# Sums of product weights from on-chip float16 parts instead of a kept float32 copy, with a new weight layout and moved steps

## Chip, cores and metric

One core of one Trainium2 chip runs the whole program. The metric is the device time of one execution in microseconds (us); before the change it is 1241.75 us, the median of three runs (1240.58 to 1242.31). The engines are TensorE (PE, with its weight loads PEld), VectorE (DVE), ScalarE (ACT), GpSimd (POOL) and SyncE (SP), which issues all DMAs here. Each engine works through its own program in order.

## The reference

Attention with a sigmoid in place of the softmax over 8 batches of 12 heads (448 positions, head size 64), whose output, as 3584 rows of 768, goes through two matrix products with an ELU between them. The two weight matrices arrive as float64.

```python
scores = scale * np.matmul(q, k.transpose(0, 1, 3, 2)) - np.log(S)
attn = 1.0 / (1.0 + np.exp(-scores))
x = np.matmul(attn, v)            # -> rows of B*S, 768 columns
h = x @ w_in                      # 768 x 2048, float64 on input
g = np.where(h > 0.0, h, np.exp(np.minimum(h, 0.0)) - 1.0)
return (g @ w_out).astype(np.float32)
```

## The kernel before

Every large product runs on float16 pairs: a value is split into a high and a low float16 part, and high x high, high x low and low x high are added up in PSUM.

**Stages in the order of time.** From 0 to about 140 us the attention of batches 0 and 1 runs while w_in arrives in eight units of 256 columns; each unit is turned from float64 words into float32 (tile `stage`) and then into float16 parts (tile `wi`). To 197 us the first layer of batch 0 runs (`ph`), to 283 us its second layer (`po`) as 96 steps X0 to X95 of three matmuls, while w_out is loaded and split (tiles `wo`, `to`, `so`). Then come the first layer of batch 1 (to about 346 us) and the attention of batch 2 (to about 442 us), with the second layer of the batch before as filling. From there on each batch 2 to 7 has a stage of blocks, in which the first layer is done by a scheme of seven products (k = 1 to 7) on half-size blocks, four times over (w = 0 to 3), 28 products n = 0 to 27 in the order of the table `USES`; then the attention of the next batch, filled with the second layer of this one. The last second layer ends the program.

**The weights of the seven products.** Three of the seven (slots 4, 5, 6 of `blend` in DRAM) are plain quarters of w_in, stored from `wi` by the step W of each unit (`store_parts`, L344, six DMAs of 96 KB). The other four are sums and differences of quarters. For them the float32 unit is stored to a DRAM tile `kept` (step t, L315, 768 KB), read back in four parts into `room` (L358, 192 KB each), added on DVE (L363), split into a high part on ACT (L369) and a low part on DVE (L372), and stored to `blend` (L379). One step K is one piece of that chain (`make_sums`); the split parts lie in a ring of three buffers, so that a fourth split waits for the store of the first.

**What sets the order.** The first stage follows a hand-written table `ORDER` of tokens: l, A to F, t are steps of a unit of w_in; S, G, V the scores, sigmoid and values of a pair of heads; X, W, K as above. `A` (L220) writes the float32 buffer of a unit, of which there are two, so A of unit u+2 waits until everything that reads unit u is done: F (L310) and the store t. The later stages follow `order`, for the first layer of batch 1, and `order_of_blocks`, which say after which product the next pair of heads is measured (`measure_next`: two reductions over the raw q, k, v on DVE and a short chain to the tile `dg`), scaled (`scale_next`: a matmul `pb` on `dg`, a short chain on DVE, then POOL) and split (`split_step`). `behind` hangs the evaluation behind each product: copies on ACT, `exps` and `rests` (the ELU), and the split of g.

Of the kernel before, what the change touches and what calls it, by code (L numbers as in the profile page):

```python
# [11 lines left out]
F32 = mybir.dt.float32  # L12
# [41 lines left out]
X79 K X80 K O4 X81 X82 K X83 K X84 X85 K X86 K X87 X88 K X89 K X90 X91 K X92 K X93 X94 K
X95 K O5
# [11 lines left out]
def attention_ffn(  # L67
# [12 lines left out]
    P = 128  # L80
# [41 lines left out]
    wi = space.rearrange("p (j c f) -> p j c f", j=2, c=NK)  # L122
    BLOCK = 2 * HK * 2 * P
    blend = dram.tile([NW, 7, P, BLOCK], F16, name="blend")
    kept = dram.tile([NF // WF, P, NK * WF * P], F32, name="kept")
# [137 lines left out]
    def load_w_in(u):  # L263

        src = w_in.rearrange("(c p) f -> p c f", p=P)
        if not stage:
            stage.append(
                sb.tile([P, WR * 2 + WT, NK, WF * P], F32, tag="wo", name="stage")
            )
        if u < NF // WF:  # L270
            st = stage[0][:, u % WR * 2 : u % WR * 2 + 2]
            st = st.rearrange("p a c x -> p (a c x)").rearrange("p (c x) -> p c x", c=NK)
            queue = nc.sync
            queue.dma_start(st.bitcast(U64), src[:, :, u * WF * P : (u + 1) * WF * P])
            w_in_words[u] = words(st)
# [3 lines left out]
    def w_in_parts(u):  # L279

        st, both = {}, w_in_both.setdefault(u // 2, {})
        d = wi[:, :, :, u * WF * P : (u + 1) * WF * P]
# [8 lines left out]
        def sums():  # L291
# [3 lines left out]
            top = st["t"].bitcast(BF16).rearrange("p a (c t) -> p a c t", t=2)[:, :, :, 1]  # L295
            for c in range(NK):
                nc.tensor.matmul(
                    to, ones_in, top[:, c], start=u % 2 == 0 and c == 0,
                    stop=c == NK - 1, skip_group_check=True,
                )  # L300
# [13 lines left out]
        def keep():  # L314
            nc.sync.dma_start(kept[u], st["t"].rearrange("p c x -> p (c x)"))  # L315

# [10 lines left out]
            "t": keep,  # L327
# [9 lines left out]
    def store_parts(u):  # L337

        w, j = divmod(u, 2)
        for slot, c, odd in ((4, 0, 0), (5, HK, 0), (6, HK, 1)):  # L340
            dst = blend[w, slot].rearrange("p (j c h x) -> p j h c x", j=2, c=HK, h=2)
            for h in range(2):
                f = (u * WF + odd) * P
                nc.sync.dma_start(dst[:, j, h], wi[:, h, c : c + HK, f : f + P])  # L344

    def sums_of_parts():

        names = "22", "21", "11", "12"
# [5 lines left out]
        def load(u, *xs):  # L354
            src = kept[u].rearrange("p (c x) -> p c x", c=NK)
            for x in xs:
                c, f = HK * (x[1] == "2"), P * (x[0] == "2")
                nc.sync.dma_start(  # L358
# [1255 lines left out]
```

## Time and profile before

| | before |
|---|---|
| median of three runs | 1241.75 us |
| the profiled execution | 1241.87 us |
| its span, first to last instruction | 1240.1 us |
| PE busy | 1130.4 us (91%) |
| DVE busy | 853.8 us (69%) |
| ACT busy | 708.6 us (57%) |
| DMA engines, mean rate | 143 GB/s |

The profiled execution takes 1.8 us more than its span, and lies 0.1 us above the median. PE has the largest share, so what counts is where PE stands idle (some 110 us) or runs below its full clock, and on what it waits there. Shares of the whole span say little: the stages have different limits.

### The profile page before, as it was taken

The numbers are of one execution on the slowest core, as the hardware profiler recorded it, in microseconds if no ns is written. First come the engines' busy times: TensorE is split into PE (matmuls) and PEld (weight loads), VectorE is DVE, ScalarE is ACT, GpSimd is POOL, SyncE is SP. The second block draws the span as 40 slices with busy tenths as digits, with TensorE's granted clock in tenths as the row PEclk, the third lists the DMA queues.
The fourth block names the chain that finished last, engine by engine and source line by source line (L and its number), as shares of the span: only waits on it lengthen the run. The fifth ranks groups of instructions, "written<-read, shape, count | busy, mean of one in ns | idle before, by whom it ended". The sixth has DMA issues, their size and how long they took to land.

```text
span 1240.1 us, 22359 instructions
## 1 busy us (share of the span) xinstructions
PE 1130.4 (91%) x8626; PEld 718.5 (58%) x8626; DVE 853.8 (69%) x1767; ACT 708.6 (57%) x983; POOL 70.0 (6%) x276
## 2 busy tenths in 40 slices
PE   6668997488998899999999998999999999999998
PEld 2223453244554479556965588557955588558965
DVE  2657787376888558787877668787877678776600
ACT  4668766153575546676566644776566545775400
POOL 0000000010000000010100000010001000010000
PEclk9889999698999999999999999999999999999999
DMA  9776647443535738443854248363844268324200
GB/s 222 195 241 203 215 130 182 127 135 115 125 102 125 215 107 251 131 99 99 255 148 104 63 141 247 105 119 121 248 129 94 57 179 259 76 62 149 89 26 26
DMA packets 258267, 177.24 MB, mean 143 GB/s; under 512 B 189552, under 2 KB 225392, under 8 KB 258160
## 3 DMA queue, kind: packets, MB, share of 16 engines
q1 hardware_dynamic: 258160, 175.82, 51.3%
q8 instruction: 67, 1.10, 0.4%
q14 instruction: 40, 0.33, 0.1%
HBM read 130.94 MB, written 28.31 MB: 128 GB/s over the span
## 4 chain that ended last, share of the span: by engine, by line
PE 59%; DVE 17%; DMA 9%; ACT 7%; SPq 4%; issue 4%; POOL 0%; DVEq 0%; ACTq 0%; POOLq 0%
PE po L1099 23%; PE psc L655 8%; PE ph L899 7%; PE pav L713 6%; PE X L998 5%; PE po_r L1099 4%; DMA qk<-nat 3%; SPq L344 2%; DVE g L1036 2%; DMA room<-kept 1%; DMA kept<-stage 1%; DMA wi<-blend 1%; PE pav L731 1%; DVE mt L211 1%; DVE wi L772 1%
## 5 line engine op out<-in xcount | busy, mean ns | idle before, releaser
L1099 PE MATMUL po<-wo,g 128*128 128x384 f16 x2304 | 392.1, 329 | 10.4 <-DVE wo L478 4.5
L1099 PEld LDWEIGHTS <-g 128*128 128x128 f16 x2688 | 258.3, 98 | 201.0 <-issue 35.8
L998 PEld LDWEIGHTS <-wi 128*128 128x128 f16 x3024 | 287.9, 98 | 28.0 <-issue 19.6
L700 DVE SCALAR_TENSOR_TENSOR at<-sg,at 128x896 f16<-128x896 f32 x126 | 132.5, 1087 | 76.9 <-ACT at L699 76.6
L998 PE MATMUL X<-wi 128*128 128x224 f16 x1296 | 133.0, 259 | 10.1 <-DVE c L1047 10.1
L679 ACT ACTIVATE sg<-psc,bias,sc 128x896 f32<-128x896 f32 x108 | 114.1, 1090 | 31.6 <-PE psc L655 31.5
L655 PE MATMUL psc<-qk 64*128 64x448 f16 (+2 forms) x960 | 110.8, 382 | 8.4 <-ACT qk L1283 3.7
L899 PE MATMUL ph<-xh,wi 128*128 128x448 f16 x576 | 114.2, 359 | 0.0
L699 ACT ACTIVATE at<-sg 128x896 f16<-128x896 f32 x126 | 113.4, 945 | 0.6
L618 ACT ACTIVATE nat<-raw,sc 128x384 f16<-128x384 f32 (+1 forms) x108 | 52.2, 535 | 79.4 <-POOL sc L589 74.5
L899 PEld LDWEIGHTS <-wi 128*128 128x128 f16 x576 | 56.7, 99 | 59.1 <-issue 8.9
L621 DVE SCALAR_TENSOR_TENSOR nat<-raw,sc,nat 128x384 f16<-128x384 f32 (+1 forms) x108 | 52.4, 526 | 28.1 <-ACT nat L618 27.4
L713 PE MATMUL pav<-at,vn 128*64 128x448 f16 x648 | 68.2, 355 | 1.1 <-DVE al L193 1.1
L1099 PE MATMUL po_r<-wo,g 128*128 128x384 f16 x384 | 64.3, 326 | 0.0
L1012 ACT ACTIVATE eb<-c,msc 128x896 f32<-128x896 f32 x24 | 25.0, 1042 | 65.4 <-DVE c L1047 65.4
L655 PEld LDWEIGHTS <-qk 64*128 64x128 f16 (+1 forms) x864 | 30.7, 98 | 53.5 <-issue 34.9
L1109 DVE TENSOR_SCALAR o<-po,osc 128x384 f32<-128x384 f32 x48 | 29.3, 611 | 41.0 <-PE po L1099 38.1
L713 PEld LDWEIGHTS <-vn 128*64 128x64 f16 x648 | 34.0, 110 | 33.3 <-issue 14.5
L998 PE MATMUL Y<-xh,wi 128*128 128x224 f16 x432 | 45.3, 259 | 2.7 <-DVE wi L772 2.7
L998 PE MATMUL X<-xh,wi 128*128 128x224 f16 x432 | 45.4, 259 | 0.8 <-DVE ea L1017 0.8
L679 ACT ACTIVATE sg<-psc,bias 128x896 f32<-128x896 f32 x42 | 41.3, 1008 | 8.3 <-PE psc L655 7.8
L998 PE MATMUL A<-xh,wi 128*128 128x224 f16 x432 | 45.3, 259 | 0.0
(162 smaller groups left out, 1396.6 us busy)
## 6 DMA issues: line engine op xcount, KB each, us to landing
wi<-blend SPq DMA_DIRECT2D x168, 384.0 KB, 4.2
stage<-in_moe_w_in_dram SPq DMA_DIRECT2D x8, 1536.0 KB, 8.7
wo<-in_moe_w_out_dram SPq DMA_DIRECT2D x13, 768.0 KB, 4.7
raw<-in_q_dram SPq DMA_DIRECT2D x96, 96.0 KB, 3.4
raw<-in_k_dram SPq DMA_DIRECT2D x96, 96.0 KB, 2.9
out_dram<-o SPq DMA_DIRECT2D x48, 192.0 KB, 1.9
rv<-in_v_dram SPq DMA_DIRECT2D x36, 192.0 KB, 2.7
kept<-stage SPq DMA_DIRECT2D x8, 768.0 KB, 5.4
```

Source lines behind the costliest of these rows:

```text
L618: nc.scalar.mul(hi, src, s)
L621: nc.vector.scalar_tensor_tensor(lo, src, s, hi, op0=ALU.mult, op1=ALU.subtract)
L655: nc.tensor.matmul(psc[:, j, :S] if g < NC else psc[rows[x], j, :S], kk[rows[j], o], qq[rows[j], :S], start=(n == 0), stop=(n == n_parts - 1),
L679: a = nc.scalar.activation(sg, psc[:, :, :S], AF.Sigmoid, bias=bias, scale=scale)
L699: nc.scalar.mul(parts[0], sg, 2.0**ATOP)
L700: nc.vector.scalar_tensor_tensor(parts[1], sg, 2.0**ATOP, parts[0], op0=ALU.mult, op1=ALU.subtract)
L713: nc.tensor.matmul(pav[rows[j], :S], vv[i][:, j * NC + g if g < NC else 2 * NC + j], sg[k][:, j], start=(g == 0 and n == 0), stop=False,)
L899: nc.tensor.matmul(ph[:, :S], wi[:, wj, c, f * P : (f + 1) * P], hidden_of(b, c)[:, xj], start=(n == 0), stop=(n == 3 * NK - 1),)
L998: nc.tensor.matmul(to[:, j * HS : (j + 1) * HS], block[:, j, c, wj], rhs(k, c, xj), start=(k in (1, 5) and j == 0 and n == 0), stop=(j == ...
L1012: a = nc.scalar.activation(e, src, AF.Exp, scale=m[:, 0, 4 * w : 4 * w + 1])
L1099: nc.tensor.matmul(po[:, :HM], lh(gj, f), wo[:, i, f, wj], start=(n == 0), stop=(n == 3 * NF - 1),)
L1109: nc.vector.tensor_scalar(o, po[:, :HM], sc, None, op0=ALU.mult)
```

## The change

- The store t and the DRAM tile `kept` are gone, and the 32 loads from it. `whole_of` adds the float16 parts of `wi` into `room` on DVE instead, 768 columns at a time, twice a unit. High and low parts are then a copy on ACT and a subtraction on DVE, without the factor. A unit has eight steps K as before; before X95 there are 29 of them instead of 31, from X14 on.
- `wi` lies by unit (last unit first), block and part. A unit of w_in comes in two DMAs (runs of 1 KB) instead of one (2 KB). W stores a unit in two DMAs with runs of 1536 bytes instead of six with 256.
- W0 to W7 stand from X62 to X91 instead of X0 to X7.
- In the stage of blocks the scaling stands after n = 5 and 17 instead of 4 and 14; the second measurement (n = 22) goes to the attention behind it, after the first pair's third sigmoid; the measurement at f = 10 in `order` goes too. The scale of the batch and the first ELU stand behind the product (1,1) instead of (2,0). The tables of Exp and Sigmoid are loaded by a one-element activation, behind (5,0) and behind the last ELU. The split of the blocked x is ordered anew (`finish_first`, `finish_second`).

```diff
-            queue.dma_start(st.bitcast(U64), src[:, :, u * WF * P : (u + 1) * WF * P])
+            for i in range(WF):
+                f = (u * WF + i) * P
+                nc.sync.dma_start(st[:, i * NK : (i + 1) * NK].bitcast(U64), src[:, :, f : f + P])
...
-        def keep():
-            nc.sync.dma_start(kept[u], st["t"].rearrange("p c x -> p (c x)"))
...
-        for slot, c, odd in ((4, 0, 0), (5, HK, 0), (6, HK, 1)):
-            dst = blend[w, slot].rearrange("p (j c h x) -> p j h c x", j=2, c=HK, h=2)
-            for h in range(2):
-                f = (u * WF + odd) * P
-                nc.sync.dma_start(dst[:, j, h], wi[:, h, c : c + HK, f : f + P])
+        for slot, n, a in ((4, 2, 0), (6, 1, 3 * HK)):
+            nc.sync.dma_start(
+                blend[w, slot : slot + n].rearrange("s p (j x) -> p s j x", j=2)[:, :, j],
+                wi[:, NU - 1 - u, a : a + n * HK].rearrange("p (s c) h x -> p s (c h x)", s=n),
+            )
...
-        def load(u, *xs):
-            src = kept[u].rearrange("p (c x) -> p c x", c=NK)
...
+        def whole_of(u, i):
+            x = room[:, 2 * i : 2 * i + 2].bitcast(F32).rearrange("p b (c x) -> p (b c) x", x=P)
+            hi, lo = (wi[:, NU - 1 - u, i * NK : (i + 1) * NK, h] for h in range(2))
+            nc.vector.tensor_tensor(x, hi, lo, op=ALU.add)
...
-            nc.scalar.mul(parts(i)[:, 0], one[x].rearrange("p (c x) -> p c x", c=HK), scale)
+            nc.scalar.copy(parts(i)[:, 0], one[x].rearrange("p (c x) -> p c x", c=HK))
...
+            elif k == 1 and w == 1:
+                first()
+                start_of_a()
             elif k == 5:
                 nc.scalar.copy(s5, bank(5, w))
+                if not w:
+                    nc.scalar.activation(warm, bias, AF.Exp)
...
             elif k == 4:
                 exps(st["e1"][:, 1], x, w)
                 rests(st["e1"][:, 1], x, w)
+                if w == NW - 1:
+                    nc.scalar.activation(warm, bias, AF.Sigmoid)
...
     order_of_blocks = {
-        4: scale_next, 7: split_step, 8: split_step, 9: split_step, 11: split_step, 12: measure_next,
-        14: scale_next, 18: split_step, 19: split_step, 20: split_step, 21: split_step, 22: measure_next,
+        5: scale_next, 7: split_step, 8: split_step, 9: split_step, 11: split_step, 12: measure_next,
+        17: scale_next, 18: split_step, 19: split_step, 20: split_step, 21: split_step,
     }
...
                 p.sigmoid(2)
+                if hp == 0:
+                    measure_next()
```

How the order of instructions moves is shown for three places. A row is the line, the operation, out<-in, the shape, and how many stand in a row.

SP, the queue that issues the DMAs, around X0 before the change (`wo` is w_out on its way in, `so` its low words):

```order
L446 DMA wo<-in_moe_w_out_dram 128x2x384 x12
L344 DMA blend<-wi 128x3x128 x48
L358 DMA room<-kept 128x3x128 x4
L446 DMA wo<-in_moe_w_out_dram 128x2x384
L1111 DMA out_dram<-o_0_0_1664 128x384
L441 DMA so_13_1708<-in_moe_w_out_dram 128x384
```

The same place in the changed kernel:

```order
L434 DMA wo<-in_moe_w_out_dram 128x2x384 x13
L1114 DMA out_dram<-o_0_0_1610 128x384
L429 DMA so_13_1652<-in_moe_w_out_dram 128x384
L1114 DMA out_dram<-o_1_0_1674 128x384
L429 DMA so_14_1681<-in_moe_w_out_dram 128x384
```

The 48 stores and four loads that stood ahead of the thirteenth load of w_out are gone from there. Further on in the same queue, from about X60, stores of sums (L373) and of the plain quarters (L338) now alternate:

```order
L373 DMA blend<-room 128x768 x2
L338 DMA blend<-wi 128x2x768
L338 DMA blend<-wi 128x768
L373 DMA blend<-room 128x768 x2
L1114 DMA out_dram<-o_0_1_1859 128x384
L338 DMA blend<-wi 128x2x768
L338 DMA blend<-wi 128x768
L338 DMA blend<-wi 128x2x768
L338 DMA blend<-wi 128x768
L373 DMA blend<-room 128x768 x2
```

So the stores of plain quarters are now queued among those of the sums on which the ring of three waits.

DVE from X62 to the scale of batch 1 (L868), before: L363 is a sum, L372 a low part, L1109 empties an output tile.

```order
L363 TENSOR_TENSOR room<-room 128x384 x2
L1109 TENSOR_SCALAR o_0_1_1914<-po_0_1_1825,osc_1399 128x384
L363 TENSOR_TENSOR room<-room 128x384 x2
L372 SCALAR_TENSOR_TENSOR room<-room,wr 128x3x128 x4
L363 TENSOR_TENSOR room<-room 128x384 x4
L372 SCALAR_TENSOR_TENSOR room<-room,wr 128x3x128 x2
L1109 TENSOR_SCALAR o_1_1_1994<-po_1_1_1908,osc_1399 128x384
L372 SCALAR_TENSOR_TENSOR room<-room,wr 128x3x128 x2
L363 TENSOR_TENSOR room<-room 128x384 x4
L372 SCALAR_TENSOR_TENSOR room<-room,wr 128x3x128 x3
L1109 TENSOR_SCALAR o_2_1_2068<-po_2_1_1987,osc_1399 128x384
L868 TENSOR_REDUCE mx_95<-xs_445 128x1
```

The same stretch after: L354 is the new `whole_of`, L357 a sum, L366 a low part, L1112 an output tile.

```order
L354 TENSOR_TENSOR room<-wi 128x768 x2
L357 TENSOR_TENSOR room<-room 128x384 x4
L366 TENSOR_TENSOR room<-room 128x3x128 x4
L354 TENSOR_TENSOR room<-wi 128x768 x2
L357 TENSOR_TENSOR room<-room 128x384 x2
L1112 TENSOR_SCALAR o_1_1_1941<-po_1_1_1851,osc_1398 128x384
L357 TENSOR_TENSOR room<-room 128x384 x2
L366 TENSOR_TENSOR room<-room 128x3x128 x4
L354 TENSOR_TENSOR room<-wi 128x768 x2
L357 TENSOR_TENSOR room<-room 128x384 x4
L366 TENSOR_TENSOR room<-room 128x3x128
L1112 TENSOR_SCALAR o_2_1_2018<-po_2_1_1935,osc_1398 128x384
```

Six instructions of 768 columns have come in, and nine low parts stand where eleven stood.

DVE in the stage of blocks of batch 4, around n = 22, before: L211 to L183 are the measurement of pair 2, L1017 and L1036 belong to the ELU and the split of g.

```order
L1017 SCALAR_TENSOR_TENSOR ea_2_7865<-X_2_7672,msc_7351,ea_2_7865 128x448
L211 TENSOR_REDUCE mx_93<-rv_97 128x1
L211 TENSOR_REDUCE mt_2_8004<-raw_2_7695 128x7
L578 TENSOR_REDUCE mx_93<-mt_2_8004 128x2
L581 TENSOR_TENSOR mx_93<-mx_93,mt_2_8004 64x1 x2
L179 STREAM_TRANSPOSE tr<-mx_93 128x32
L181 TENSOR_REDUCE trm<-tr 128x1
L183 TENSOR_SCALAR dg<-blocks,trm 128x12
L1036 SCALAR_TENSOR_TENSOR g<-eb_2_7942,msc_7351,g 128x4x224
L1016 TENSOR_SCALAR ea_3_8057<-ea_3_8057 128x448
```

After the change those rows stand behind the stage of blocks, in the attention (L688 is the second half of a sigmoid):

```order
L1031 SCALAR_TENSOR_TENSOR g<-eb_3_8049,msc_7309,g 128x4x224
L1031 SCALAR_TENSOR_TENSOR g<-ea_3_8000,msc_7309,g 128x2x224
L688 SCALAR_TENSOR_TENSOR at_0_8118<-sg_0_8091,at_0_8118 128x896
L688 SCALAR_TENSOR_TENSOR at_0_8121<-sg_0_8116,at_0_8121 128x896
L210 TENSOR_REDUCE mx_92<-rv_96 128x1
L210 TENSOR_REDUCE mt_2_8152<-raw_2_7651 128x7
L566 TENSOR_REDUCE mx_92<-mt_2_8152 128x2
L569 TENSOR_TENSOR mx_92<-mx_92,mt_2_8152 64x1 x2
L178 STREAM_TRANSPOSE tr<-mx_92 128x32
L180 TENSOR_REDUCE trm<-tr 128x1
L182 TENSOR_SCALAR dg<-blocks,trm 128x12
```

The measurement no longer splits the evaluation of the blocks; it now stands between the sigmoids of the first pair.

## Rows read from the trace of the kernel before

**Rows 1.** Windows: length, busy PE, PEld, DVE, ACT, POOL, PE clock, DMA share, GB/s

```profile
60.00:80.00 20.00, 12.15 (x54) 3.85 (x51) 9.30 (x15) 10.77 (x10) 0.00 (x0) 0.83 0.95 289
200.00:220.00 20.00, 8.97 (x51) 4.75 (x50) 10.66 (x18) 6.70 (x12) 0.00 (x0) 0.89 0.90 190
220.00:240.00 20.00, 4.50 (x17) 2.21 (x17) 5.55 (x10) 4.10 (x7) 0.00 (x0) 0.52 0.48 131
```

**Rows 2.** Timeline of ACT: start, duration, line, operation [idle before <-releaser]

```profile
51.50 1.58 ACT L220 ACTIVATE stage<-stage 128x1536 f32<-128x1536 f32 x1 [5.60 <-DMA kept<-stage]
...
64.12 1.01 ACT L679 ACTIVATE sg<-psc,bias 128x896 f32<-128x896 f32 x1 [0.21 <-PE psc L655]
...
71.85 1.58 ACT L220 ACTIVATE stage<-stage 128x1536 f32<-128x1536 f32 x1 [6.72 <-DMA kept<-stage]
```

**Rows 3.** Timeline of DVE and of PE in the same stretch

```profile
45.03 1.82 DVE L310 SCALAR_TENSOR_TENSOR wi<-stage,swi,wi 128x1536 f16<-128x1536 f32 x1 [0.62 <-ACT wi L325]
...
74.39 1.86 PE L655 MATMUL psc<-early 64*128 64x448 f32 x4 [6.82 <-ACT sg L679]
```

**Rows 4.** Timeline of SP's queue: start and duration of issuing

```profile
61.35 0.54 SPq L315 DMA_DIRECT2D kept<-stage  x1
...
195.84 27.83 SPq L344 DMA_DIRECT2D blend<-wi  x48
...
226.53 0.42 SPq L446 DMA_DIRECT2D wo<-in_moe_w_out_dram  x1
```

**Rows 5.** Timeline of DVE, PE and ACT around X0

```profile
204.38 0.96 DVE L249 SCALAR_TENSOR_TENSOR wo<-wo 128x768 uint32<-128x768 uint32 x1
...
210.25 2.48 PE L1099 MATMUL po<-wo,g 128*128 128x384 f16 x14 [1.07 <-DVE wo L478]
...
232.81 0.88 ACT L228 ACTIVATE wo<-wo 128x768 uint32<-128x768 uint16 x1 [23.67 <-DMA wo<-in_moe_w_out_dram]
...
235.50 0.80 PE L242 MATMUL so<-wo,ones 128*128 128x384 bf16 x2 [22.77 <-DVE wo L233]
236.10 4.71 PE L1099 MATMUL po<-wo,g 128*128 128x384 f16 x18
```

**Rows 6.** DMA issues of the whole kernel: count, KB each, median us to landing

```profile
wo<-in_moe_w_out_dram SPq DMA_DIRECT2D x13, 768.0 KB, 4.7
...
blend<-room SPq DMA_DIRECT2D x32, 192.0 KB, 2.1
```

**Rows 7.** Timeline of PE from X62 to the scale of batch 1

```profile
267.03 16.62 PE L1099 MATMUL po<-wo,g 128*128 128x384 f16 x101 [0.18 <-DVE wo L478]
...
291.37 0.17 PE L189 MATMUL pb<-dg,ones 128*128 128x4 bf16 x1 [4.32 <-DVE dg L183]
```

**Rows 8.** Groups by line and shape: count, busy us, mean ns, idle before

```profile
L363 DVE TENSOR_TENSOR room<-room 128x384 f32<-128x384 f32 x32 | 17.8, 556 | 30.4 <-DMA room<-kept 29.9
```

**Rows 9.** Timeline of PE and ACT in the attention of batch 2

```profile
391.93 2.05 PE L1099 MATMUL po<-wo,g 128*128 128x384 f16 x9 [3.39 <-DVE o L1109]
...
405.61 0.61 ACT L369 ACTIVATE room<-room,wr 128x384 f16<-128x384 f32 x1 [5.70 <-issue]
```

**Rows 10.** What PE waits for, 546 to 1092 us: total, times, longest

```profile
PE X L998 <- DVE c L1047: 8.1, 4, 2.1
PE pb L189 <- DVE dg L183: 8.0, 8, 1.5
```

**Rows 11.** Timeline of batch 4's blocks and the attention behind them: DVE, ACT, PE

```profile
747.20 0.68 DVE L211 TENSOR_REDUCE mx<-rv 128x1 f32<-128x512 f32 x1
...
749.92 0.23 DVE L183 TENSOR_SCALAR dg<-blocks,trm 128x12 bf16<-128x12 bf16 x1
...
779.26 1.28 ACT L679 ACT_TABLE_LOAD   x1
...
783.51 2.09 DVE L700 SCALAR_TENSOR_TENSOR at<-sg,at 128x896 f16<-128x896 f32 x2 [3.20 <-ACT at L699]
...
786.22 0.17 PE L189 MATMUL pb<-dg,ones 128*128 128x12 bf16 x1
```

More of the change, by code (lines that the diff above doesn't have):

```diff
@@ L56 @@
+h16 p15 p16 X60 h17 X61 h18 p17 p18 X62 K W0 X63 X64 K O3 X65 K X66 W1 X67 K X68 K X69
+X70 K W2 X71 K X72 X73 K X74 K W3 X75 X76 K X77 K X78 W4 X79 K X80 K O4 X81 X82 K W5 X83
+K X84 X85 K X86 K W6 X87 X88 K X89 K X90 W7 X91 K X92 K X93 X94 K X95 K O5
 """
@@ L267, in load_w_in @@
             stage.append(
-                sb.tile([P, WR * 2 + WT, NK, WF * P], F32, tag="wo", name="stage")
+                sb.tile([P, WR * 2 + WT, WF * NK, P], F32, tag="wo", name="stage")
             )
@@ L368, in high @@
         def high(x, i):
-            nc.scalar.mul(parts(i)[:, 0], one[x].rearrange("p (c x) -> p c x", c=HK), scale)
+            nc.scalar.copy(parts(i)[:, 0], one[x].rearrange("p (c x) -> p c x", c=HK))
         def low(x, i):
-            nc.vector.scalar_tensor_tensor(
-                parts(i)[:, 1], one[x].rearrange("p (c x) -> p c x", c=HK), scale,
-                parts(i)[:, 0], op0=ALU.mult, op1=ALU.subtract,
+            nc.vector.tensor_tensor(
+                parts(i)[:, 1], one[x].rearrange("p (c x) -> p c x", c=HK), parts(i)[:, 0],
+                op=ALU.subtract,
             )
@@ L381, in store @@
             )
-        load(0, *names)
-        yield
-        n_u = NF // WF
-        for u in range(n_u):
-            scale = wr[:, u * WF : u * WF + 1]
+        for u in range(NU):
             i = 4 * u
-            ahead = load if u < n_u - 1 else lambda *_: None
+            whole_of(u, 0)
+            yield
+            whole_of(u, 1)
+            yield
             add("22", "21", "22", ALU.add)
@@ L818, in finish_first @@
         one.blend_rows(0)
-        blended(one.b, one.xs, slice(1, HK), slice(2 * HS, 3 * HS))
-    def finish_second(one, two):
+        blended_high(one.xs, c, x)
         one.low_rows()
@@ L825, in finish_second @@
             one.blend_rows(i)
+        blended_low(one.xs, c, x)
+    def finish_second(one, two):
         two.low_rows()
@@ L828, in finish_second @@
             two.blend_rows(i)
[L829 removed]
+        blended(one.xs, slice(1, HK), slice(0, 2 * HS))
         one.greatest()
@@ L1061, in behind @@
             elif k == 2:
-                if not w:
-                    first()
-                st["e1"] = sb.tile([P, 2, S], F32, tag="sg", name=f"ea{b}_{w}", bufs=SB)
-                exps(st["e1"][:, 0], bank(2, w), w)
-                rests(st["e1"][:, 0], bank(2, w), w)
                 if w:
+                    start_of_a(w)
                     parts_of_g(w - 1, 1)
```

95 lines of the change are left out of this document (44 added, 51 removed).

## The prediction

> **What bounds the kernel now.** I read the page first: TensorE (PE) is busy for 91% of the span, so that about 110 us are idle, and a change is worth what it takes from these or from stretches at the low clock. Then the windows of 20 us: PE does 12.15 us of work at 60 to 80, 8.97 at 200 to 220 and only 4.50 at 220 to 240, with a granted clock of 0.52 of full speed there, which is nearly the lower of its two levels (1.2 of 2.4 GHz) [rows 1]. So I looked up, in the timelines of each engine, what ended the idle time in these windows. From 546 us on no such hole is left; what PE waits for there stands in the waits by line.
>
> In the first stage two steps A stand still until a store to `kept` has landed, for 5.60 and 6.72 us [rows 2], and PE waits behind the second of them, through ACT's sigmoid, for 6.82 us [rows 3]. Around 210 us SP spends 27.83 us on issuing the 48 stores W before it comes to the thirteenth load of w_out, at 226.53 [rows 4]. ACT waits 23.67 us for that load, and PE 22.77 us for what follows [rows 5]. The stage of blocks has small waits only: in four batches 8.1 us for the add of product (7,w) and 8.0 us for `dg` [rows 10].
>
> **The change part by part, in us saved.**
>
> *Kept stores.* Without the store the first A needs F (L310), which ends at 45.03 + 1.82 = 46.85 [rows 3], and starts at once instead of at 51.50: 4.6. The second is then held only by ACT, free at 64.12 + 1.01 = 65.13 instead of 71.85 [rows 2]: 6.7. Together 11.3 at best. But from 60 to 80 the DMA engines are 0.95 busy at 289 GB/s [rows 1]; if all they carry there is needed at once, the second wait can shrink by no more than the time of the 768 KB store that goes, 0.79 MB / 289 GB/s = 2.7, which leaves 4.6 + 2.7 = 7.3. SP issues w_in in twice as many DMAs with runs half as long, which costs a part too. I take 10, with 6 and 11.3 for the bounds.
>
> *W moved.* Now the thirteenth load waits only for its buffer, released by DVE at 204.38 + 0.96 = 205.3 [rows 5]. With the 6.3 that it took here (226.53 to 232.81) it lands at 211.6, with the usual 4.7 [rows 6] at 210.0. From its landing to PE's matmul it is 235.50 - 232.81 = 2.7, so 212.7 to 214.3, and PE has work until 210.25 + 2.48 = 212.7 [rows 5]. A wait of 0 to 1.6 is left of 22.77; I take 0.9, a gain of 21.9. The hole has a tail: after it 18 matmuls take 4.71, at 0.165 each (16.62 / 101 [rows 7]) they would take 3.0, so 1.7 more, of which I count 1.1 since 1.6 of wait might still be there. Sum +23, bounds 21 and 24.5.
>
> *235 to 267.* One cast and one low part more stand in the chain of ACT and DVE that splits w_out, about 0.6 lost; the loads of `so` are no longer behind other loads, up to 3 gained, I count 1.2. +0.6, bounds -1 and 3.
>
> *X62 to the scale of batch 1.* Here DVE is the slower one already: PE waits 4.32 for `dg` at 291.37 [rows 7]. Before, DVE has 12 sums and 11 low parts, three output tiles and the chain of 0.8. With 0.556 each for the sums [rows 8] and 0.6 for low parts and tiles this is 6.7 + 6.6 + 1.8 + 0.8 = 15.9, in the 24.3 us from 267.0 to 291.3 [rows 7]: some 8 us are waits for loads of `room` and for the ring of three. After, it has six `whole_of`, 12 sums, nine low parts. No row shows a `whole_of`. It lies between a sum of half as many columns, 0.556, and the 0.96 that 768 columns took in L249 [rows 5, 8]; I take the upper one, since 768 columns are its row. So 5.8 + 6.7 + 5.0 + 1.8 + 0.8 = 20.1. The Trainium skill (VectorE: DVE Perf Modes, "The perf-mode tier table (the rule you actually need)") grants a tensor-tensor operation the double rate only if every tensor has 16 bits, which the float32 result excludes; by it the sum is the same 20.1, by the double rate it would be some 2.4 less, and no run shown here has the operation.
>
> The waits for loads are gone, those for the ring are not: two fourth low parts fall into the stretch. A store of sums lands in 2.1 [rows 6], but now up to two W stand ahead of it in the queue, 0.59 MB each, 2.0 us at 289 GB/s. That makes about 2.8 for each wait, the cast included, 5.6 in all: 25.7 us, 1.4 more than before. If the W go on at the rate of before, 48 x 96 KB in 27.83 us or 170 GB/s [rows 4], each takes 3.5 and the loss is up to 7; without any contention 1.5 is gained. I take -2, since the rate is not known. On this the Trainium skill (DMA: Bandwidth & Descriptors, "Specifications") says that transfers reach the line rate from 512 bytes on, and pay a read-modify-write below; W goes from 256 to 1536. By it the rate is the higher one, and the loss near 1; the trace shows 190 GB/s at 0.90 busy in the window of W [rows 1], which agrees as far as it goes.
>
> *First layer of batch 1.* Four `whole_of` come in, a measurement goes, and PE is busy throughout: 0.
>
> *Attention of batch 2.* The wait of 3.39 behind a load of `room` goes; ACT's 5.70 at a sum's cast [rows 9] goes mostly too. Against it stand waits for the ring, and a `pb` that now waits for the moved measurement. -0.5, from -4 to 3.
>
> *Blocks.* The measurement takes 747.20 to 750.15, 2.95 [rows 11]. It stood in DVE's way at n = 22, and (4,3) waited for the add behind it; the scaling at 14 waited for the one at 12. Both waits, and 0.5 of `Y` and of the first `pb`, 4 us a batch [rows 10], seem to go. I don't count them: DVE has work in every gap of this stage, scaling at 17 brings the split at 18 behind POOL, and the copy that (7,3) needs stands behind that split on ACT. So about 1 each for (1,3), (7,3), (4,3) comes back: 0.4 gained of 4. In the attention behind it the measurement stands after two sigmoid parts of DVE that end at 783.51 + 2.09 = 785.6. The table of Sigmoid, 1.28 [rows 11], loads earlier, and the blocks end 0.4 earlier, so they end at 783.9 then and `dg` is ready at 783.9 + 2.95 = 786.9, while PE reaches `pb` at 786.22 - 0.4 = 785.8: a new wait of 1.1, or none if PE's filling work runs late. So between -0.7 and 0.4 in each of five batches, I take -0.4, and 1 us gained in the last, which has no attention behind it: -1, bounds -4 and 3. Work on POOL and the new order of splitting x I cost at nothing: they lie beside filling products of PE; without these each costs its own length, under 1 us a batch.
>
> Sum: 10 + 23 + 0.6 - 2 + 0 - 0.5 - 1 = 30.1. The profiled execution took 1241.87, 0.1 over the median, so 1211.8, or 1212.
>
> **The rivals.**
> - *The first stage gives little.* The waits on `kept` turn into waits for q, k, v or w_in in a queue that is full from 60 to 80 [rows 1]. 2 instead of 10 are gained: 1220. Against it: from 40 to 60 the queue has room, and the first wait lies there.
> - *The waits in the blocks do go.* For it speaks that each has a cause which is moved away [rows 10, 11]; 4 us in each of six batches instead of -1: 1187.
> - *The sums hold up the output tiles.* W at 170 GB/s, and ring waits that go on into the first layer of batch 1: 7 to 9 us back, 1219.
> - *Slower than before.* SP's queue carries W and the sums in the same stretch. The longest landing of a store seen is 71.85 - 61.35 = 10.5 [rows 2, 4], against 2.1. Each of three ring waits at that price gives 25 back, 1237; only from 10 us on for each, or with a fourth such wait, the whole 30 is used up, 1242 to 1246. Against it: the queue was at 0.48 to 0.90 around the W of before [rows 1].
>
> **How the numbers follow.** A measurement of this kernel tells about 0.2%, or 2.5 us, from no change. The forecast has 0.60, the rivals in turn 0.14, 0.11, 0.11 and 0.04, of which the last gives 0.02 to no change. The bounds of the terms, added as independent, give about 7 on either side of 1212; with the first and third rival the range goes to 1226, and below to 1199, which leaves out the blocks' rival and the slower one, 0.15 together, and some of the tails. Faster 0.95, same 0.02, slower 0.03.
>
> **What would show it.** In the profile after, no wait of L220 on a DMA store; windows at 40 to 80 with 3 to 5 us more of PE work each; the hole after 210 us gone, with `so` at once or within 2 us, and the clock there at 0.9 or more; PE's wait for `dg` before the first layer of batch 1 at 4 to 8 us, with ring waits on `blend<-room` in front of it; and in the blocks no wait for `dg` at n = 12 but waits of about 1 us at (1,3), (7,3) and (4,3), and one at the first `pb` of the attention behind. The forecast fails if the first window shows the same wait under another name, if the W stores land late enough for the DVE chain to lose over 10 us, or if PE's waits from 546 to 1092 us sink to a few us.

## The result and the profile after

The changed kernel takes 1209.28 us (median of four, 1208.14 to 1213.12), against 1241.16 us for the kernel before beside it: a ratio of 0.975, 95% interval 0.9725 to 0.9775. The forecast was 1212, from 1199 to 1226. The profiled execution took 1208.79 us with a span of 1207.0.

The page's first part shows what moved: PE has the same work, 93% of a shorter span, and the work on DVE has grown by 12 us.

```profile
PE 1128.0 (93%) x8626; PEld 719.1 (60%) x8626; DVE 865.7 (72%) x1783; ACT 706.8 (59%) x996; POOL 65.3 (5%) x276
```

The windows that answer to [rows 1], and the stretch of the W stores in the new place (columns as there):

```profile
60.00:80.00 20.00, 15.78 (x91) 5.95 (x89) 14.79 (x25) 16.46 (x17) 0.18 (x1) 1.00 0.82 221
...
200.00:220.00 20.00, 16.17 (x96) 9.16 (x94) 12.73 (x26) 5.33 (x12) 0.87 (x2) 1.00 0.30 90
220.00:240.00 20.00, 18.84 (x101) 10.27 (x101) 17.21 (x31) 11.57 (x23) 2.44 (x4) 0.91 0.49 175
229.00:255.00 26.00, 21.20 (x125) 12.20 (x125) 21.39 (x40) 6.67 (x13) 0.00 (x0) 0.98 0.78 281
```

From 60 to 80 PE has 15.78 us of work instead of 12.15, with the clock at 1.00 instead of 0.83; from 40 to 60 it has 14.73 instead of 11.94, a little under the 3 to 5 us more that the prediction named as a sign. The hole at 200 to 240 is gone, and the clock there is 1.00 and 0.91 instead of 0.89 and 0.52.

To say where the time went I cut every execution at the same points of the program: the first matmul of the first layer of batch 0 (`ph`), of its second layer (`po`), of batch 1's first layer, of batch 2's attention (`psc`), and the first product into `Y` of each batch's blocks. The starts are read in PE's timeline; a stage is the difference of two starts.

| us | before | after | saved | forecast |
|---|---|---|---|---|
| to the first layer of batch 0 | 139.66 | 126.96 | 12.7 | 10 |
| first layer of batch 0 | 58.43 | 58.44 | 0 | 0 |
| second layer of batch 0 (W, w_out) | 85.39 | 61.60 | 23.8 | 23.6 |
| first layer of batch 1 (its `pb`) | 62.31 | 62.25 | 0.1 | -2 |
| attention of batch 2, to `Y` | 104.50 | 109.77 | -5.3 | -0.5 |
| batches 2 to 6, from `Y` to `Y` | 675.17 | 674.10 | 1.1 | -2 |
| from batch 7's `Y` to the end | 114.64 | 113.88 | 0.8 | 1 |
| span | 1240.1 | 1207.0 | 33.1 | 30.1 |

The first stage is the one length that differs between executions of the same code: in the twelve profiles in which it is unchanged it is 126.3 to 129.6. The kernel before has one profile only, so its own scatter there is not known. Where the code is the same, the first layer of batch 0 repeats within 0.01, the three stages after it within 1.2 to 1.7 us, and the sum over batches 2 to 6 within 0.2 in eight profiles (673.9 to 674.1) but only within 0.7 in runs 10 and 11. So profiles settle differences that the medians of the times do not.

ACT's step A no longer waits for a DMA; it starts at 45.65 and 59.27, where it started at 51.50 and 71.85 [rows 2]:

```profile
45.65 1.59 ACT L219 ACTIVATE stage<-stage 128x1536 f32<-128x1536 f32 x1 [0.99 <-DVE wi L311]
...
59.27 1.59 ACT L219 ACTIVATE stage<-stage 128x1536 f32<-128x1536 f32 x1
```

ACT after the thirteenth load of w_out has a wait of 0.69 us, and PE goes from one group of 14 matmuls to `so` without a gap (ACT first, then PE):

```profile
197.11 0.91 ACT L227 ACTIVATE wo<-wo 128x768 uint32<-128x768 uint16 x1 [0.69 <-DMA wo<-in_moe_w_out_dram]
```

```profile
197.54 2.48 PE L1102 MATMUL po<-wo,g 128*128 128x384 f16 x14 [1.07 <-DVE wo L466]
199.87 0.50 PE L241 MATMUL so<-wo,ones 128*128 128x384 bf16 x2
200.21 3.09 PE L1102 MATMUL po<-wo,g 128*128 128x384 f16 x18
```

What PE waits for from X62 to the middle of batch 2's attention:

```profile
230.55 16.61 PE L1102 MATMUL po<-wo,g 128*128 128x384 f16 x101 [0.19 <-DVE wo L466]
...
255.08 0.17 PE L188 MATMUL pb<-dg,ones 128*128 128x4 bf16 x1 [4.51 <-DVE dg L182]
...
325.05 0.17 PE L188 MATMUL pb<-dg,ones 128*128 128x12 bf16 x1 [3.04 <-DVE dg L182]
325.07 6.71 PE L1102 MATMUL po<-wo,g 128*128 128x384 f16 x30
...
357.95 0.17 PE L188 MATMUL pb<-dg,ones 128*128 128x12 bf16 x1 [4.39 <-DVE room L366]
357.97 7.70 PE L1102 MATMUL po_r<-wo,g 128*128 128x384 f16 x30
```

The wait for `dg` in the first layer of batch 1 stays, 4.51 after 4.32 [rows 7]. The ring of three shows in front of it as two waits of DVE:

```profile
239.57 0.56 DVE L366 TENSOR_TENSOR room<-room 128x384 f16<-128x384 f32 x1 [1.57 <-ACT room L363]
...
248.44 0.56 DVE L366 TENSOR_TENSOR room<-room 128x384 f16<-128x384 f32 x1 [2.27 <-ACT room L363]
```

The two waits at 325 and 357 are new; each is followed by 30 matmuls that take 6.71 and 7.70 us. The same 30 took 5.04 in the kernel before:

```profile
356.83 5.04 PE L1099 MATMUL po<-wo,g 128*128 128x384 f16 x30
...
383.51 5.04 PE L1099 MATMUL po_r<-wo,g 128*128 128x384 f16 x30
```

Taken over the whole attention of batch 2 (before, then after), PE's idle time grows from 9.0 to 11.3 us, and the same 696 matmuls take 98.46 instead of 95.54 us at a mean clock of 0.94 instead of 0.97. So more than half of the 5.3 us lost is the slower clock and not waiting:

```profile
345.80:450.29 104.49, 95.54 (x696) 51.23 (x696) 71.38 (x149) 62.68 (x85) 6.51 (x26) 0.97 0.50 135
```

```profile
309.25:419.02 109.77, 98.46 (x696) 52.43 (x696) 81.13 (x170) 63.91 (x90) 7.80 (x26) 0.94 0.41 116
```

What stands behind the wait at 357 shows in SP's queue, on ACT and on DVE:

```profile
347.13 1.55 SPq L614 DMA_TRANSPOSE qk<-nat  x1
348.74 1.76 SPq L496 DMA_DIRECT2D raw<-in_q_dram  x2
...
353.83 0.62 SPq L524 DMA_DIRECT2D rv<-in_v_dram  x1
354.50 3.80 SPq L373 DMA_DIRECT2D blend<-room  x4
```

```profile
356.85 0.51 ACT L363 CAST room<-room 128x384 f16<-128x384 f32 x1 [5.76 <-DMA blend<-room]
357.27 0.63 ACT L733 ACTIVATE wi<-pav,xs 128x448 f32<-128x448 f32 x1
```

```profile
351.39 0.23 DVE L182 TENSOR_SCALAR dg<-blocks,trm 128x12 bf16<-128x12 bf16 x1
```

SP issues the transpose and the eight loads of a pair, 7.4 us, and only then, at 354.50, the stores of sums. ACT's cast, the fourth split of the ring, waits 5.76 us for the first of them. PE's 4.39 do not hang on `dg`, which was done at 351.62, nor on the low part (L366) that the row names: `pb` waits for ACT as well, and shares its PSUM buffer with `pav` (`pb_tag` in the code). ACT empties `pav` with L733, which stands right behind the cast and ends at 357.90, and `pb` starts at 357.95.

PE's waits in four of the later batches, which answer to [rows 10]:

```profile
PE X L993 <- DVE ea L1012: 7.7, 8, 1.2
PE X L993 <- DVE c L1042: 5.4, 4, 1.4
PE pb L188 <- DVE dg L182: 3.0, 4, 0.8
PE X L993 <- ACT B L1063: 2.0, 4, 0.5
```

They have other names and places, and are 18.1 us in all. Before they were 18.6, the two of [rows 10] and these:

```profile
PE Y L998 <- DVE wi L772: 1.8, 4, 0.5
PE X L998 <- DVE ea L1017: 0.7, 4, 0.2
```

After the change 7.7 are at (1,2) and (1,3), which wait for the ELU on DVE, 5.4 at (4,3), 2.0 at (7,3) and 3.0 at the first `pb` of the attention.

### The profile page after: what moved, and what is told of

The parts are those of the page before. It is cut to its first block, busy times and chain, and to the rows that moved or that the text cites. A ratio compares the mean times of both kernels' runs of the same rounds, so it can differ in the third digit from the quotient of the medians.

```text
span 1207.0 us, 22288 instructions
## 1 busy us (share of the span) xinstructions
PE 1128.0 (93%) x8626; PEld 719.1 (60%) x8626; DVE 865.7 (72%) x1783; ACT 706.8 (59%) x996; POOL 65.3 (5%) x276
## 4 chain that ended last, share of the span: by engine, by line
PE 58%; DVE 20%; ACT 9%; DMA 6%; issue 4%; SPq 2%; POOL 1%; DVEq 0%; ACTq 0%; POOLq 0%
PE po L1102 22%; PE psc L643 7%; PE pav L701 6%; PE X L993 6%; PE po_r L1102 5%; PE ph L894 4%; DVE g L1031 2%; PE A L993 2%; PE Y L993 2%; ACT sg L667 2%; DMA vn<-in_v_dram 1%; PE pav L719 1%; DVE ea L1012 1%; PE B L993 1%; DVE nat L609 1%
## 5 line engine op out<-in xcount | busy, mean ns | idle before, releaser
L688 DVE SCALAR_TENSOR_TENSOR at<-sg,at 128x896 f16<-128x896 f32 x126 | 132.5, 1087 | 62.3 <-ACT at L687 62.0
L1102 PE MATMUL po_r<-wo,g 128*128 128x384 f16 x384 | 67.1, 335 | 0.0
L1112 DVE TENSOR_SCALAR o<-po,osc 128x384 f32<-128x384 f32 x48 | 29.3, 611 | 41.6 <-PE po L1102 38.6
L1031 DVE SCALAR_TENSOR_TENSOR g<-ea,msc,g 128x448 f16<-128x448 f32 x48 | 32.5, 678 | 17.8 <-ACT g L1026 17.8
```

Source lines behind the costliest of these rows:

```text
L688: nc.vector.scalar_tensor_tensor(parts[1], sg, 2.0**ATOP, parts[0], op0=ALU.mult, op1=ALU.subtract)
L1031: nc.vector.scalar_tensor_tensor(rows_of_g(w, 1, odd, lo, hi), x, gs, rows_of_g(w, 0, odd, lo, hi), op0=ALU.mult, op1=ALU.subtract,)
L1102: nc.tensor.matmul(po[:, :HM], lh(gj, f), wo[:, i, f, wj], start=(n == 0), stop=(n == 3 * NF - 1),)
L1112: nc.vector.tensor_scalar(o, po[:, :HM], sc, None, op0=ALU.mult)
```

## The experiments

All of them change the changed kernel. The table has the stages in which they differ, read as above, and the ratio to the kernel before, timed on the same chip.

| run | 2nd layer b0 | 1st layer b1 | attention b2 | batches 2 to 6 | median us | ratio (95%) |
|---|---|---|---|---|---|---|
| after | 61.60 | 62.25 | 109.77 | 674.1 | 1209.28 | 0.975 (0.9725 to 0.9775) |
| 1 dead kept stores | 61.28 | 62.25 | 109.84 | 674.0 | 1223.35 | 0.9837 (0.9805 to 0.9868) |
| 2 measurement of batch 2 | 61.79 | 62.25 | 105.61 | 674.0 | 1206.66 | 0.971 (0.9677 to 0.9743) |
| 3 sums by GpSimd | 61.65 | 65.66 | 99.11 | 673.9 | 1202.65 | 0.967 (0.9639 to 0.9702) |
| 4 W in front | 68.86 | 60.02 | 108.24 | 674.0 | 1215.17 | 0.9789 (0.9745 to 0.9833) |
| 5 W in small pieces | 61.76 | 69.88 | 108.81 | 674.1 | 1216.60 | 0.9773 (0.973 to 0.9816) |
| 6 measurement at 22 | 61.78 | 62.19 | 106.05 | 693.4 | 1224.69 | 0.9843 (0.98 to 0.9886) |
| 7 scaling at 4, 14 | 61.92 | 62.03 | 110.08 | 663.7 | 1198.56 | 0.9626 (0.9598 to 0.9654) |
| 8 run 2 + GpSimd late | 61.54 | 60.74 | 99.39 | 674.0 | 1199.94 | 0.9636 (0.9584 to 0.9688) |
| 9 run 8 + W later | 61.97 | 61.31 | 99.94 | 674.0 | 1199.08 | 0.9631 (0.9589 to 0.9673) |
| 10 scaling at 5, 15 | 62.48 | 61.50 | 108.40 | 665.9 | 1202.53 | 0.9663 (0.963 to 0.9697) |
| 11 runs 8 and 10 | 61.42 | 62.18 | 100.24 | 666.6 | 1192.48 | 0.9573 (0.9546 to 0.96) |
| 12 run 11, scaling at 4, 15 | 61.77 | 62.04 | 99.89 | 661.8 | 1187.41 | 0.9564 (0.9542 to 0.9587) |

**1. The kept stores, dead.**

```diff
+            "t": lambda: nc.sync.dma_start(kept[u], st["t"].rearrange("p c x -> p (c x)")),
```

> The changed kernel with the eight stores of the float32 units put back at their old places in SP's queue; nothing reads them. Theory: the landing of these stores is what held step A, so ACT waits 4 to 7 us twice on them again, the first layer of batch 0 begins 11 to 13 us later, and the time is 1220 to 1223 us. Rival: the first stage became shorter because w_in now comes in two DMAs a unit and lies by block; then the dead stores cost under 4 us, 1209 to 1213.

The first layer of batch 0 began at 142.16, 15.2 us later than after the change and 12.5 to 15.8 later than in the other profiles. ACT waits on the stores again:

```profile
53.30 1.58 ACT L192 ACTIVATE stage<-stage 128x1536 f32<-128x1536 f32 x1 [7.09 <-DMA kept<-stage]
...
74.47 1.58 ACT L192 ACTIVATE stage<-stage 128x1536 f32<-128x1536 f32 x1 [7.27 <-DMA kept<-stage]
```

The theory holds: the dead stores cost all that the stage had gained, so within the 3 us by which it varies nothing of it came from how w_in is loaded. The time (1223.35) is just over its range.

**2. The measurement of batch 2.**

```diff
-    order = {1: [scale_next], 3: [split_next], 4: [measure_next], 6: [scale_next], 8: [split_next]}
+    order = {1: [scale_next], 3: [split_next], 4: [measure_next], 6: [scale_next], 8: [split_next], 10: [measure_next]}
...
-                if hp == 0:
+                if hp == 0 and b > 2:
                     measure_next()
```

> The changed kernel with one measurement put back: that of pair 2 of batch 2, beside column block 10 of the first layer of batch 1 as before; the later batches keep the new place. Theory: the 3.04 us that PE waits for dg in the first pair of batch 2 come from the moved measurement, and so does the slow clock behind it (30 matmuls in 6.71 us instead of 5.04); both go, 1204 to 1206 us. Rival: ACT and DVE come out of the first layer late anyway, and the measurement only shifts that; 1208 to 1211.

The attention of batch 2 is 4.2 us shorter, and no other stage changes: the first layer of batch 1 takes the measurement in at no cost. The wait of 3.04 and the slow matmuls behind it are gone, the time is a little over the range (1206.66). But the rival had a point: other waits came instead, 0.61 at the second `pb` and 0.92 at `psc`, and the one behind the ring grew from 4.39 to 5.32. PE's idle time falls by 0.3 us only, to 11.0; the other 3.8 us are matmuls at a mean clock of 0.97 instead of 0.94.

```profile
358.13 0.17 PE L188 MATMUL pb<-dg,ones 128*128 128x12 bf16 x1 [5.32 <-DVE room L366]
```

```profile
311.38:416.99 105.61, 94.65 (x696) 51.41 (x696) 78.57 (x162) 63.65 (x90) 7.80 (x26) 0.97 0.43 121
```

**3. The stores of sums from GpSimd.**

```diff
         def store(u, x, i):
             w, j = divmod(u, 2)
-            nc.sync.dma_start(
+            nc.gpsimd.dma_start(
```

> The changed kernel with the 32 stores of sums issued from GpSimd's queue instead of SP's. Theory: the ring of three waits for stores that are ready but stand in SP's queue behind a transposing DMA and eight loads, so the wait of 4.39 us at dg in the third pair of batch 2 goes with the slow clock behind it (30 matmuls in 7.70 us instead of 5.04), and a part of the 4.51 us ahead of the first layer of batch 1: 1201 to 1204 us. Rival: DVE is late there by its own work, or the stores by the traffic; then the waits stay within 2 us of what they are, 1207 to 1211.

The attention of batch 2 falls by 10.7 us, more than expected, and no wait of `pb` behind a ring store is left in it. Not all of that is the ring's: the wait for the moved measurement, too, is 1.34 instead of 3.04. The other half was wrong: the wait in the first layer of batch 1 grew to 8.03.

```profile
260.58 0.16 PE L188 MATMUL pb<-dg,ones 128*128 128x4 bf16 x1 [8.03 <-DVE dg L182]
...
327.17 0.17 PE L188 MATMUL pb<-dg,ones 128*128 128x12 bf16 x1 [1.34 <-DVE dg L182]
```

DVE's two ring waits in front of the first are 3.77 and 3.60 us instead of 1.57 and 2.27, 3.5 more together. A store from GpSimd lands in 3.0 us (median) instead of 1.9, which makes 2.2 of them; where the rest comes from is not shown. So SP's order cost time in the attention, and not ahead of it, where SP issues only W and output tiles beside the sums.

**4 and 5. Place and size of W.** Run 4 puts W0 to W7 back behind X0 to X7; run 5 leaves them and stores small pieces:

```diff
-        for slot, n, a in ((4, 2, 0), (6, 1, 3 * HK)):
...
+        for slot, a in ((4, 0), (5, HK), (6, 3 * HK)):
+            dst = blend[w, slot].rearrange("p (j c h x) -> p j h c x", j=2, c=HK, h=2)
+            for h in range(2):
+                nc.sync.dma_start(dst[:, j, h], wi[:, NU - 1 - u, a : a + HK, h])
```

> The changed kernel with W0 to W7 back behind X0 to X7, still as 16 large DMAs. Theory: the place counts: the thirteenth load of w_out stands behind 16 issues (8 us) and 4.7 MB of stores, some 16 us at 289 GB/s, so PE waits 8 to 16 us again near 200 us, and gets back some 1.5 us ahead of the first layer of batch 1: 1215 to 1224 us. Rival: the piece size was the cause, large pieces hide behind the load that is on its way anyway: a wait below 3 us, 1207 to 1212.

> The changed kernel with W0 to W7 at the new places, X62 to X91, but each again as six DMAs of 96 KB with runs of 256 bytes. Theory: the size counts as much as the place: 48 issues of 0.58 us stand among the stores of sums, each W takes 3.5 us instead of 2, and the ring of three waits for it; the stretch from X62 to the scale of batch 1 grows by 10 to 20 us, 1219 to 1230 us. Rival: the place alone counted; 4 us at most, 1209 to 1213.

Run 4: SP needs 13.28 us for the 16 issues, the load comes at 197.32, and PE waits 5.80 (SP, then PE):

```profile
183.93 13.28 SPq L310 DMA_DIRECT2D blend<-wi  x16
197.32 0.72 SPq L406 DMA_DIRECT2D wo<-in_moe_w_out_dram  x1
```

```profile
206.74 0.80 PE L213 MATMUL so<-wo,ones 128*128 128x384 bf16 x2 [5.80 <-DVE wo L204]
```

The second layer of batch 0 is 7.3 us longer than after the change (the first layer of batch 1 gets 2.2 of it back), and 16.5 shorter than before it. So of the 23.8 us the larger pieces bring 16.5 at the old place (with the four loads from `kept` that are gone), and the move after them 7.3. The wait was smaller than expected, since the stores ran faster than the 289 GB/s that I had reckoned with. It also helped that SP began them at 183.93, 9.6 us before DVE released the buffer of that load (192.60 + 0.96 = 193.56). The window while they run (run 4, columns as in [rows 1]):

```profile
190.00:197.00 7.00, 4.31 (x24) 2.17 (x23) 6.96 (x13) 4.88 (x10) 0.00 (x0) 1.00 1.07 396
```

Run 5: at the new place the small pieces cost 7.6 us in the first layer of batch 1, less than expected and more than the rival allows. With small pieces the move brings 23.6 in the second layer of batch 0 and loses these 7.6, so 16.0: either half alone brings some 16 us, and which of them counts for more depends on the order in which they are taken. DVE waits for the ring for 6.2 us twice, and the rate falls to 207 GB/s from the 281 of the changed kernel (the timeline of DVE, then the window):

```profile
244.70 0.56 DVE L365 TENSOR_TENSOR room<-room 128x384 f16<-128x384 f32 x1 [6.18 <-ACT room L362]
...
257.44 0.56 DVE L365 TENSOR_TENSOR room<-room 128x384 f16<-128x384 f32 x1 [6.15 <-ACT room L362]
```

```profile
229.00:264.00 35.00, 21.54 (x128) 12.30 (x126) 21.90 (x41) 7.08 (x14) 0.00 (x0) 0.87 0.85 207
```

**6. The measurement at n = 22.** In every batch, with the one at column block 10 as in run 2.

```diff
-        17: scale_next, 18: split_step, 19: split_step, 20: split_step, 21: split_step,
+        17: scale_next, 18: split_step, 19: split_step, 20: split_step, 21: split_step, 22: measure_next,
...
-                if hp == 0:
-                    measure_next()
```

> The second measurement back at n = 22 in the blocks of every batch (and at column block 10 of the first layer of batch 1), all else as changed; to be read beside the version with only the measurement of batch 2 put back, 1206.7 us. Theory: DVE is full in the blocks, so the wait at (4,3) grows to about 2 us and the one of 0.7 at the first pb of the attention goes; the two cancel, 1205 to 1208 us. Rival: the move was worth 2 us a batch, hidden by a loss elsewhere in the change: 1214 to 1218.

The theory falls, and the rival's 2 us a batch are too few (1224.69). Each of five batches is 3.5 to 4.3 us longer than in run 2. The wait at (4,3) is 4.3 us instead of 1.4, the one at the attention's `pb` (0.8) goes, and the matmuls behind the longer wait run slowly, 18 in 3.52 us, for which 1.89 are usual (PE):

```profile
600.12 3.52 PE L993 MATMUL X<-wi 128*128 128x224 f16 x18 [4.26 <-DVE c L1042]
```

So the move of the measurement is worth some 4 us a batch beside a scaling at 17. Since the change as a whole gained 0.2 there, its other parts taken alone lose nearly as much.

**7 and 10. The scaling.** Run 7 has it behind n = 4 and 14 as before the change, run 10 behind 5 and 15.

```diff
-        5: scale_next, 7: split_step, 8: split_step, 9: split_step, 11: split_step, 12: measure_next,
-        17: scale_next, 18: split_step, 19: split_step, 20: split_step, 21: split_step,
+        4: scale_next, 7: split_step, 8: split_step, 9: split_step, 11: split_step, 12: measure_next,
+        14: scale_next, 18: split_step, 19: split_step, 20: split_step, 21: split_step,
```

> The changed kernel with the two scalings in the blocks back behind n = 4 and 14 (the measurement stays in the attention). Theory after the last runs: it is the scaling at 17 that brings the split behind it late, and with it the copy for (7,3) and DVE's adds for (4,3); at 14 these waits (0.5 and 1.3 us a batch) go and a part of the 1.1 at (1,3), while pb waits 1.3 to 1.8 us for dg again; 1 to 1.5 us gained in each of five batches, 1201 to 1205 us. Rival: DVE is full wherever the steps stand, and the waits only change their names: 1207 to 1211.

> The changed kernel with the second scaling behind n = 15 instead of 17. Theory: one product later than 14 dg is ready, so pb waits for nothing, and the split at 18 still comes in time; the waits at (7,3) and (4,3) go for nothing in return, 1.8 to 2.6 us in each of five batches, 1196 to 1201 us. Rival: as in the run above, 1207 to 1211.

Run 7 gains 2.0 to 2.2 us in each of five batches, more than expected. Of the waits at (1,2), (1,3), (7,3) and (4,3) only 0.2 at (1,3) is left, against `pb` waits of 1.6 and 0.7 us for `dg`:

```profile
PE pb L188 <- DVE dg L182: 8.6, 8, 1.6
PE pb L188 <- DVE al L192: 1.1, 4, 0.3
PE X L993 <- DVE ea L1012: 0.7, 4, 0.2
```

Run 10 has no wait for `dg` at the second scaling, but keeps 0.8 at (1,2) and 1.0 at (1,3), and gains 1.6 a batch: less than run 7, and with 8.2 us in all less than the 9 that I had set as its least; the time, 1202.53, lies over its range.

**8, 9, 11 and 12. Together.** Run 8 joins run 2 with GpSimd's stores from batch 2's attention on; run 9 also puts W beside column blocks 1 to 8 of the first layer of batch 1; run 11 is run 8 with the scaling at 5 and 15, and run 12 with 4 and 15.

```diff
         def store(u, x, i):
             w, j = divmod(u, 2)
-            nc.sync.dma_start(
+            queue = nc.gpsimd if late else nc.sync
+            queue.dma_start(
...
             for hp in range(NP):
+                if b == 2 and not hp:
+                    late.append(1)
```

> The changed kernel with the measurement of pair 2 of batch 2 put back, and the stores of sums issued by GpSimd from the attention of batch 2 on only (before that by SP). Theory: the two losses of that attention are apart, 4.2 us for the measurement and 10.7 us at most for stores that stand behind loads in SP's queue, and GpSimd's slower stores hurt only ahead of the first layer of batch 1; the attention takes 96 to 99 us instead of 109.8, 1195 to 1200 us. Rival: the two are one wait, and 1202 to 1205 stays.

> As the run above, and W0 to W7 moved on, to column blocks 1 to 8 of the first layer of batch 1. Theory: W in SP's queue between X62 and X91 delays the stores of sums on which the ring waits; without it the stretch to the scale of batch 1 is 2 to 3 us shorter: 1192 to 1198 us. Rival: the ring waits there are those of three buffers, not of the queue, and W now delays the stores of the first layer: no gain, 1196 to 1201.

> The changed kernel with three edits that each run of its own spoke for: the measurement of pair 2 of batch 2 back beside the first layer of batch 1, the stores of sums by GpSimd from the attention of batch 2 on, the second scaling behind n = 15. Theory: the places are apart, so the gains add up: 1199.9 less 9 to 13, 1187 to 1191 us. Rival: the attention behind the blocks takes the gain back, 1195 to 1200.

> As the last run (measurement of batch 2 put back, stores of sums by GpSimd from the attention of batch 2 on, second scaling behind n = 15), with the first scaling behind n = 4 as before the change. Theory: the 0.8 us that PE waits at (1,2) with the scaling behind 5, and had not with 4 and 14, come from the first scaling; it goes, and the wait for dg that 14 had stays away: blocks and attention of batches 2 to 6 take 660 to 663 us instead of 666.6, 1186 to 1190 us. Rival: DVE is full, and the 0.8 us come back at (1,3) or (4,3): 1191 to 1194.

Run 8's time met its theory, and the first layer of batch 1 keeps SP's quicker stores. Its attention takes 99.39, just over the range, and no less than in run 3 (99.11), where the measurement stood at its new place; so the 4.2 of run 2 and the 10.7 of run 3 do not add up there. As run 3 has 3.4 us more of waiting in the layer ahead, in which DVE may catch up, the price of the ring alone is read from run 8 against run 2: 6.2. Run 9 brought nothing (60.74 to 61.31 in that layer): without W in the queue PE's wait for `dg` in the first layer of batch 1 is 3.89 instead of 4.50, so W accounts for 0.6 us of it at most. Run 11 came out above its range at 1192.48; its stages are those of its parts within 1.5 us, but 2.9 more in all. Run 12 is the best of all, 0.9564 of the time before: with the first scaling at 4 the wait at (1,2) is gone, and only 0.3 a batch at `pb` came in its place (the row for `al`).

```profile
PE X L995 <- DVE ea L1014: 3.5, 4, 1.0
PE pb L188 <- DVE dg L182: 3.0, 4, 0.8
PE pb L188 <- DVE al L192: 1.1, 4, 0.3
PE X L995 <- DVE c L1044: 0.9, 3, 0.6
```

## Why the forecast was right

*Kept stores, 10.* Right in its mechanism, as run 1 shows. The size was too low: 12.7 in the profile, 11.6 against the mean of the twelve, both over its upper bound of 11.3. What I held back for a full queue wasn't needed (0.82 busy at 60 to 80 after the change), and the slow clock behind each wait, which I had not counted, came back too: 0.83 instead of 0.74 at 40 to 60 and 1.00 instead of 0.83 at 60 to 80.

*W, 23.* Right, 23.8 together with the 0.6 of the stretch behind it. The wait left over is 0 on PE, the lower bound. Runs 4 and 5 add what the trace of before couldn't tell: the size of the pieces alone brings some 16 us, as the place alone does, and the forecast had put all of it down to the place in the queue.

*X62 to the scale of batch 1, -2.* Too careful: 0.2 was lost. From X62 to `pb` it took 24.5 us, 24.3 before, and not 25.7, because the waits for the ring were 1.57 and 2.27 us and not 2.8 each. In the sum nine low parts are 5.0, that is 0.556 each and not the 0.6 named beside it; they took 0.552. The `whole_of` took the upper bound:

```profile
L354 DVE TENSOR_TENSOR room<-wi 128x768 f32<-128x768 f16 x16 | 14.9, 952 | 0.1
```

The Trainium skill's rule for tensor-tensor operations, that the double rate needs every tensor to have 16 bits (VectorE: DVE Perf Modes, "What auto-detection actually checks"), agrees: with a float32 result no doubled rate, 952 ns for 768 columns, where a sum of 384 takes 556. The Trainium skill's rule that transfers reach the line rate from 512 bytes on (DMA: Bandwidth & Descriptors, "Specifications") agrees as far as the runs go: with runs of 1536 bytes 396 GB/s (run 4) and 281 GB/s at a DMA share of 0.78 (the changed kernel), with 256 bytes 207 at 0.85 (run 5). No run has a size between, so where the limit lies is not shown here.

*Attention of batch 2, -0.5, from -4 to 3.* This step failed: 5.3 lost. I had named both causes and priced them too low. The moved measurement costs 4.2 there (run 2): the wait is 3.04, and 1.7 are the slow matmuls behind it (30 in 6.71 instead of 5.04), but with it gone other waits come, and what is gained is nearly all clock. The forecast had no term for the clock behind a new wait. For the ring I counted landings, and not the place in the queue: a store stands behind the transpose and the eight loads of a pair, 7.4 us of issuing, and what it holds up on ACT is the copy that frees `pb`'s buffer. Without that 6.2 more are gained (run 8 against run 2).

*Blocks, -1.* The sum was off by 2.8 us, and the steps were right: the waits at n = 12, at (4,3) and for `Y` go, new ones come at (1,3), (7,3), (4,3) and at the first `pb` (1.2, 0.5, 1.4 and 0.8 in batch 3's blocks and behind them), and one at (1,2), 0.8, that I had not named. The working has a slip: three waits of about 1 out of 4 leave 1, and not 0.4. And I gave "DVE has work in every gap" as a reason that nothing could be gained, beside the true one. Runs 6, 7 and 12 refute it: the measurement's move is worth some 4 us a batch beside the scaling at 17, and 2.3 at most beside the one at 4 and 14 (run 7 against before, with the other moves in the blocks), the scaling at 5 and 17 takes 2 of them back, and with 4 and 15 each batch is some 2.5 us shorter than after the change. So the rival that had these waits go was half right about what the move could give, and the order of the scaling was the reason why it didn't.

Of the other rivals, the first stage's was refuted by the trace after the change (12.7 gained; of ACT's waits from 40 to 80 only 0.8 us is for a DMA, a load of w_in), that of the sums and the slower one by the trace, in which the ring waits stayed under 2.3 us before the first layer of batch 1. So the sum was close in part by luck: the terms that were too low (first stage, X62, blocks, 7.6 together) and the one that was too high (batch 2, 4.8) partly cancelled.

What stays open: which of the moves inside the blocks besides the measurement and the scaling (first ELU behind (1,1), tables loaded early, new order of splitting x) brings the 0.5 us at `Y` and at the first `pb` of the blocks; they weren't run apart.

## What to carry to other kernels

A wait for a transfer is read in the queue that issues it: before its landing time is counted, count what stands ahead of it in that engine's program, waiting instructions and issue times included. A full engine doesn't mean that moving its work is worth nothing: what matters is which of its results is late, so measure each move alone, because two moves that are made together can hide each other. And compare executions stage by stage: a stage that mostly repeats within 0.2 us, as the blocks here, tells differences that the total hides. And a wait can cost more than its length, as in the attention of batch 2, where the 30 matmuls behind it took 6.71 us instead of 5.04; so compare the time of the same matmuls too.

## What the runs showed of the hardware

With stores of 1536-byte runs and hardly anything else the DMA engines moved 396 GB/s for 7 us (run 4), well above the 289 that I had taken from the kernel before for a full queue. A store of 192 KB issued by GpSimd landed in 3.0 us (median) instead of 1.9; with all of them moved off SP the first layer of batch 1 was 3.4 us longer, where SP had little else to issue, and the attention behind it 10.7 shorter. And in that attention the same 696 matmuls took 92.5 us at a mean clock of 1.00 (run 8) and 98.5 at 0.94 (after the change).
